# The first batch of a polysketch attention kernel: k turned without stride, v loaded by token group on two queues, remainders on 128 rows

## The chip, the core and the metric

The kernel runs on one core of a Trainium2 chip. The metric is device time in microseconds for one execution; the time given is the median of several runs. The engines are named as the profile names them: PE (TensorE; PEld for its weight loads), DVE (VectorE), ACT (ScalarE), POOL (GpSimd) and SP (SyncE, which here only issues DMAs). ACT can issue DMAs as well.

## What is computed

Attention with a polynomial sketch, and behind it a feed-forward layer with squared ReLU. There are 4 batches, 4 heads, 1088 tokens and head size 32, with 8 sketch rows.

```
def phi(x):
    a = np.einsum('rd,bhsd->bhsr', S1, x)
    b = np.einsum('rd,bhsd->bhsr', S2, x)
    return np.einsum('bhsi,bhsj->bhsij', a, b).reshape(*x.shape[:-1], r * r)
q_p, k_p = (phi(q), phi(k))
kv = np.einsum('bhsf,bhsd->bhfd', k_p, v)
z = np.sum(k_p, axis=2)
num = np.einsum('bhsf,bhfd->bhsd', q_p, kv)
den = np.einsum('bhsf,bhf->bhs', q_p, z)[..., None] + 1e-06
x = (num / den)            # to (4352, 128): a token's four heads side by side
h = np.maximum(x @ w_in, 0.0)        # 128 -> 2048
out = h * h @ w_out                  # 2048 -> 128
```

## The kernel before, in words

**The feed-forward part** sets most of the time. The 4352 tokens are cut into nine chunks: two of 512 tokens for each batch (32 rows of tokens times 16), and one of 256 for the remainders (2 tokens of each row of 34). For each chunk there are 16 steps. A step is a first product, `pg` (L938: 128 columns of w_in with xT, the normalized attention turned so that features lie on partitions), a squared ReLU shared among DVE, ACT and POOL, and a second product, `po` (L1026), summed over the 16 steps. The call `block()` (L1005) emits one first product, four steps ahead, and one second product; a block is the unit in which the code counts time, in `now`.

**The attention part** gives xT. For a batch, k and q are turned 32 by 32 on DVE (`turned`, L237), projected on the sketches (`proj` for the first batch, `proj4` for the others), and spread to 64 features by an outer product of the two factors (`outer`, on DVE or POOL). `KvRows` (L423) sums k's features with v on PE, and the sums z of the features from the factors alone (`factor_sums`). `keep_rows` (L455) copies the first from PSUM by ACT, `turn`, `place`, `pick_sums` and `own_sums` set both into the operand `kvbd` of `numerators` (L499). `normalize_first` or `normalize` divides and scales on DVE, and the result is turned on PE (x_ps) or through DRAM into xT.

**The first batch's first group** is written out by hand (L1035 to L1130), because the feed-forward part can't begin without it. Its order on each engine is the order of the code. `idle_products` are products of zeros with no use but to keep PE at work. `first_two` (L963) emits the first two first products of chunk 0.

**The loads** stand in SP's queue in the order of the code (L164 to L183). For batch 0: k in two halves (each of four groups of 128 columns), k's remainder, q's first half, v by heads (four loads to 128 partitions), q's second half, v's remainder in two loads, then w_in, w_out and batch 1. The sketches go out on ACT's queue. Each element of xt, and each partition of v_sb, stands for a set of tokens; the transposition of k writes with a stride, so that its columns agree with v's partitions. v's remainder and k's are kept for two batches in one tile, each on 64 partitions.

**Everything later** is emitted by generators, called lanes. After each block `pump` lets each lane that is due make one step. A lane holds itself back by conditions on `now`, on an estimate of when DVE and POOL are free (`dve_free`, `pool_free`), and on a flag that one buffer of PSUM is taken (`take_nd`). `second_group` makes chunk 1 (batch 0, second group); `batch_gen` makes batches 1 to 3, each with two chunks. A batch's factors of q go out to DRAM and come back as f (`factors_gen`, SP's queue). A chunk that is made more than 12 blocks ahead of its use goes through DRAM: `x<-xsT` (L643), and three blocks later four loads `xT<-x` (L649), also on SP's queue. `first_product` asks for a chunk when its first step is due: chunk c in block 16c - 2.

Of the kernel before, what the change touches and what calls it, by code (L numbers as in the profile page):

```python
# [21 lines left out]
def kernel(  # L22
# [24 lines left out]
    VONE = H * 8 * D  # L47
# [33 lines left out]
    for b in range(B):  # L81
        for x, tag in ((k_sb, "k_sb"), (q_sb, "q_sb")):
            x[b] = cpool.tile([128, NM * D], F32, name=f"{tag}{b}")
        v_sb[b] = cpool.tile([128, VONE + D], F32, name=f"v_sb{b}")
    for r in range(2):
        v_rm[r] = cpool.tile([128, H * D + D], F32, name=f"v_rm{r}")
# [33 lines left out]
    def load_v(b, h):  # L120
        sp.dma_start(  # L121
            v_sb[b][:, 256 * h : 256 * h + 256],
            bass.AP(
                v.tensor,
                v.offset + (b * H + h) * S * D,
                [[NM * D, 32], [8 * D, 4], [1, 8 * D]],
            ),
        )

    def load_v_rest(b, i):  # L130
        sp.dma_start(
            _v(v_rm[b // 2], 0, [[D, H], [1, D]], 64 * (b % 2) + 32 * i, 32),
            bass.AP(
                v.tensor,
                v.offset + (b * H * S + 32 + i) * D,
                [[NM * D, 32], [S * D, H], [1, D]],
            ),
        )
# [26 lines left out]
    load_k(0, 1)  # L165
    load_rest(k_sb[0], k, 0)
    load_q(0, 0)
    for h in range(H):
        load_v(0, h)
    load_q(0, 1)  # L170
    for i in range(2):
        load_v_rest(0, i)
# [7 lines left out]
    for i in range(2):  # L180
        load_v_rest(1, i)
# [9 lines left out]
    warm = cpool.tile([1, 2], F32)  # L191
    dve.memset(warm[:], 0.0)
    act.activation(warm[:, 1:2], warm[:, 0:1], Square)
# [9 lines left out]
    for i in range(B):  # L203
        (dve if i == 0 else pool).memset(kvbd[i][:], 0.0)
    for b in range(B):
        pool.memset(v_sb[b][:, VONE : VONE + D], 1.0)
    for r in range(2):
        pool.memset(v_rm[r][:, H * D : H * D + D], 1.0)
# [19 lines left out]
    def idle_products(n, w=512):  # L228
        idle_ps = pspool.tile([128, 512], F32, name="idle_ps", tag="po", bufs=2)
        for i in range(n):  # L230
            nc.tensor.matmul(idle_ps[:, 0:w], zero[:, 0:128], zero[:, 0:w])  # L231
# [5 lines left out]
    def turned(x, g, of_q=False):  # L237

        if g < 2:
            xt = apool.tile([128, 512], F32, tag="xt", bufs=6)  # L240
            c0, w = (512 * g, 128) if of_q else (128 * g, 256)
            dve.transpose(  # L242
                xt[:, :] if of_q else _v(xt, 0, [[128, 4], [1, 4], [4, 32]]),
                _v(x, c0, [[32, 4], [w, 4], [1, 32]]),
            )
# [108 lines left out]
    rest_ab = {}  # L354
    for r in range(2):
        rest_ab[r] = (
            cpool.tile([128, 64], F32, name=f"abr{r}"),
            cpool.tile([128, 256], F32, name=f"phr_k{r}"),
        )

    def proj_rests(xk, b, xqs, qf=None, ps_tag="ms"):
# [5 lines left out]
        for g, xt in xqs:  # L367
            nc.tensor.matmul(ab_ps[64 * g : 64 * g + 64, 64:128], w_bt[:, :], xt[:, 0:64])
        act.copy(
            _v(rest_ab[b // 2][0], 0, [[32, 2], [8, 4], [1, 8]], p0, 64),  # L370
# [6 lines left out]
    def outer_rest(b, eng, a=None):  # L377
        p0 = 64 * (b % 2)
        ab, ph = rest_ab[b // 2]
# [7 lines left out]
    def factor_sums(ps, c0, ab, a0, a1, w, p0, n, first, last):  # L387

        nc.tensor.matmul(
            ps[32 * w : 32 * w + 32, c0 : c0 + 32],  # L390
            ab[p0 : p0 + n, a0 : a0 + 32],
            ab[p0 : p0 + n, a0 + a1 : a0 + a1 + 32],
            start=first,
            stop=last,
        )
# [27 lines left out]
    class KvRows:  # L423
# [3 lines left out]
        def __init__(self, b, abs_=None):  # L427
            self.b, self.abs = b, abs_
            self.ps = pspool.tile([128, 1024], F32, name="kvr_ps", tag="nd", bufs=1)

        def values(self, ph, c0, vt, v0, v1, p0, n, first, last):
            for h in range(H):
                nc.tensor.matmul(  # L433
                    self.ps[32 * h : 32 * h + 32, 0:64],
                    vt[p0 : p0 + n, v0 + v1 * h : v0 + v1 * h + 32],
                    ph[p0 : p0 + n, c0 + 64 * h : c0 + 64 * h + 64],
# [4 lines left out]
        def tile(self, ph, g, t, last=False):  # L441
            self.values(
                ph, 256 * t, v_sb[self.b], D * (4 * g + t), 256, 0, 128, g + t == 0, last
            )

        def rest(self, last=False):
            r, p0 = self.b // 2, 64 * (self.b % 2)
            self.values(rest_ab[r][1], 0, v_rm[r], 0, D, p0, 64, False, last)

        def rest_sums(self):  # L450
            factor_sums(
                self.ps, 512, rest_ab[self.b // 2][0], 0, 32, 0, 64 * (self.b % 2), 64, False, True
            )
# [5 lines left out]
        def keep_sums(self):  # L459
            self.sums = apool.tile([128, 32], F32, name="kvz", tag="kvz")  # L460
            act.copy(self.sums[:, :], self.ps[:, 512:544])

        def products(self, phs):
            for g in range(2):
                for t in range(4):
                    self.tile(phs[g], g, t)
                for t in range(4):
                    factor_sums(
                        self.ps, 512, self.abs, 128 * g + 32 * t, 256, t, 0, 128,
                        g == 0, g == 1 and t > 0,  # L470
                    )
            self.rest(True)
# [19 lines left out]
        def spread(self):  # L492
# [4 lines left out]
            own_sums(self.b, t_ps, 64)  # L497
# [34 lines left out]
    def normalize_first(nds, xT):  # L532


        (den, rden, top, rtop, rs), (_, mp, _, beta) = norm_tiles()
        xs = apool.tile([128, 512], F16, tag="xs")
        for i, nd in enumerate(nds):
# [10 lines left out]
        dve.tensor_tensor(out=rtop[:, :], in0=top[:, :], in1=rden[:, :], op=mult)  # L548

        mm, rm = (_v(nds[1], 144 + 8 * x, [[1, 4]]) for x in range(2))  # L550
        dve.tensor_reduce(
            out=mm, in_=_v(rtop, 0, [[4, 4], [1, 4]]),
            axis=AX, op=amax, apply_absolute_value=True,
        )
        dve.tensor_scalar(
            out=mp[:, :], in0=mm, scalar1=1.0, scalar2=1.0 / 1024.0, op0=add, op1=mult,
        )
        dve.reciprocal(rm, mp[:, :])
        dve.tensor_tensor(
            out=_v(rs, 0, [[4, 4], [1, 4]]),  # L560
            in0=_v(rden, 0, [[4, 4], [1, 4]]),
            in1=_v(nds[1], 152, [[1, 4], [0, 4]]),
            op=mult,
# [8 lines left out]
        yield  # L572
        pool.tensor_tensor(out=beta[:, :], in0=mp[:, :], in1=mp[:, :], op=mult)
# [181 lines left out]
    def batch_gen(b):  # L755
# [55 lines left out]
        kv.spread()  # L811
# [223 lines left out]
    idle_products(7)  # L1035
    s_ps = pspool.tile([128, 16], F32, name="s_ps", tag="nd", bufs=1)
    nc.tensor.transpose(s_ps[:, :], s_nat[:, :], iden[0:16, 0:16])
    idle_products(4, 128)
    xk = [turned(k_sb[0], 0)]
# [5 lines left out]
    )  # L1045
    for x in range(2):
# [7 lines left out]
    phq = ph_tile("ph_q", 2)  # L1054
    xkr = turned(k_sb[0], 2)
    xq = turned(q_sb[0], 0, True)
# [5 lines left out]
    kv0 = KvRows(0)  # L1062
    for g in range(2):
        for t in range(4):
            factor_sums(kv0.ps, 512, pk[g][1], 32 * t, 128, t, 0, 128, g == 0, g == 1 and t > 0)
# [9 lines left out]
    pick_sums(zt_ps, 0, kv0.sums)  # L1075
    for t in range(4):
        kv0.tile(phk[1], 1, t)
    own_sums(0, zt_ps, 0)
    xq1 = turned(q_sb[0], 1, True)
# [17 lines left out]
    kv0.rest(True)  # L1097
    kv0.keep_rows()
    pqT = [turned_half(phq, 0, (act, act))]
# [3 lines left out]
    pqT.append(turned_half(phq, 2, (act, dve)))  # L1103
# [5 lines left out]
    pq1 = proj(xq1, "pg")  # L1109
    phq1 = ph_tile("ph_q", 2)  # L1110
    xT0 = apool.tile([128, 512], F16, name="xT", tag="xT", bufs=3)
    norm = normalize_first(nd0, xT0)
    next(norm)
    for t0 in (0, 2):
        outer(phq1, pq1[1], t0, 2, pool)
# [4 lines left out]
    idle_products(4)  # L1120
    chunk_of(0, 0, xT0, next(norm))
    first_two()
    pqT = [turned_half(phq1, 0, (act, dve))]
# [10 lines left out]
    def second_group():  # L1134
        pqT.append(turned_half(phq1, 2, (act, dve)))
        yield 1, 0
# [6 lines left out]
    lanes.append([second_group(), 1, 1])  # L1143
    add_work(*(batch_gen(b) for b in range(1, B)))
    later = []
    for b in range(2, B):
# [4 lines left out]
        later += [(n + 6 + i, load_v_rest, (b, i)) for i in range(2)]  # L1151
# [40 lines left out]
```

## Time and profile before

| | |
|---|---|
| median of 3 runs | 195.96 us (195.68 to 195.97) |
| the profiled execution | 196.73 us, its span 194.8 us |
| PE busy | 185.4 us (95%), 1380 products |
| DVE, ACT, POOL busy | 119.6, 108.2, 71.1 us |
| chain that ended last | PE 89%, SP's queue 3%, DMA 2%, ACT 2% |
| DMA in the first 20 us | share 0.85 of 16 engines, 264 GB/s |
| first second product (po, L1026) | 19.92 us |
| last one's end, PE (po_r, L985) | near 191 us |

Times inside a profile count from the first instruction of the span. A row of the timeline merges instructions of one line; its bracket gives the idle time before it and who ended it. A wait for several semaphores is put down to the one that came last by the profile. "issue" in the chain is time in which an engine waited for nothing that the profile shows.

### The profile page before, as it was taken

To read this page: it belongs to the slowest core of one execution; us is meant where nothing else is said; L and a number is where in the kernel's file an instruction comes from. 1 tells how busy PE (TensorE), PEld (TensorE's weight loads), DVE (VectorE), ACT (ScalarE), POOL (GpSimd) and SP (SyncE) were. 2 spreads that over 40 slices of the span, in tenths; PEclk is the share of its full clock that TensorE was granted. 3 is DMA by queue.
4 is the path that set the end of the run, shared out by engine and by line. 5 is a ranking of instruction groups with operands and counts; after the bars stand their busy time and mean duration, and the time that the engine had idled before them with its cause. 6 is when DMAs were issued, how large, how long until landed. Compare 5 with 4: busy or idle time off the path is not lost.

```text
span 194.8 us, 3746 instructions
## 1 busy us (share of the span) xinstructions
PE 185.4 (95%) x1380; PEld 97.2 (50%) x1380; DVE 119.6 (61%) x272; ACT 108.2 (56%) x212; POOL 71.1 (36%) x91
## 2 busy tenths in 40 slices
PE   7985999999999999999999999999999999999992
PEld 2763445454545454545454455554454444444791
DVE  4956495556487848455877545567558664644671
ACT  3235659655466755544766655457646565456570
POOL 3604122645236229242370654542524222522200
PEclk9999999999999999999999999999999999999999
DMA  6799380298913837649130349199100411300021
GB/s 170 212 347 313 107 298 25 59 242 279 228 16 108 253 69 177 192 94 280 27 54 1 52 96 263 42 227 231 29 3 0 84 30 13 54 0 2 5 52 27
DMA packets 37826, 23.17 MB, mean 119 GB/s; under 512 B 27888, under 2 KB 33264, under 8 KB 37808
## 3 DMA queue, kind: packets, MB, share of 16 engines
q1 hardware_dynamic: 37568, 22.86, 45.2%
q8 instruction: 11, 0.18, 0.4%
q14 instruction: 7, 0.06, 0.2%
q10 hardware_dynamic: 240, 0.07, 0.2%
HBM read 16.26 MB, written 6.67 MB: 118 GB/s over the span
## 4 chain that ended last, share of the span: by engine, by line
PE 89%; SPq 3%; DMA 2%; issue 2%; ACT 2%; DVE 1%; DVEq 0%
PE po L1026 56%; PE pg L938 16%; PE nd L257 4%; PE kvr_ps L433 2%; DMA v_rm<-in_v_dram 2%; PE po L985 2%; PE po_r L985 2%; PE ab_ps L257 2%; PE ab_ps L276 1%; SPq L121 1%; PE t_ps L1085 1%; PE idle_ps L231 1%; SPq L105 1%; SPq L95 0%; ACT phTh L74 0%
## 5 line engine op out<-in xcount | busy, mean ns | idle before, releaser
L1026 PE MATMUL po<-g,w_o 128*128 128x512 f32 x256 | 130.7, 592 | 0.1
L955 DVE TENSOR_SCALAR gt<-pg 128x512 f32<-128x512 f32 (+1 forms) x105 | 67.5, 647 | 50.8 <-PE pg L938 42.9
L958 ACT ACTIVATE g<-gt 128x512 f32<-128x512 f32 (+1 forms) x105 | 62.5, 597 | 60.8 <-DVE gt L955 58.8
L1026 PEld LDWEIGHTS po<-g,w_o 128*128 128x128 f32 x256 | 48.5, 191 | 39.7 <-issue 19.7
L938 PE MATMUL pg<-xT,w_in 128*128 128x512 f16 x126 | 47.7, 380 | 1.0 <-DVE own_z L409 0.8
L946 POOL TENSOR_TENSOR g<-gt 128x512 f32<-128x512 f32 x22 | 22.9, 1039 | 70.1 <-ACT gt L945 70.1
L938 PEld LDWEIGHTS <-w_in 128*128 128x128 f16 x142 | 13.9, 98 | 28.1 <-issue 27.1
L326 POOL TENSOR_TENSOR phF<-f,f 128x576 f32<-128x576 f32 (+1 forms) x12 | 16.1, 1364 | 10.7 <-DMA f<-q_two 10.7
L344 POOL TENSOR_TENSOR ph_k<-ab 128x512 f32<-128x512 f32 x14 | 14.5, 1068 | 8.9 <-ACT ab L282 7.7
L945 ACT ACTIVATE gt<-pg 128x512 f32<-128x512 f32 x22 | 12.8, 581 | 0.1
L911 POOL TENSOR_TENSOR o_sb<-oT,beta_t 128x512 f32<-128x512 f32 x8 | 8.4, 1048 | 9.7 <-DVE oT L906 4.0
L952 ACT ACTIVATE g<-gt 128x512 f32<-128x512 f32 x15 | 9.4, 630 | 0.5
L242 DVE STREAM_TRANSPOSE xt<-k_sb 128x512 f32<-128x512 f32 x8 | 8.3, 1106 | 1.4 <-DMA k_sb<-in_k_dram 1.4
L257 PEld LDWEIGHTS nd<-kvbd,phF 128*64 128x64 f32 x208 | 6.9, 137 | 4.5 <-issue 3.8
L951 ACT ACTIVATE gt<-pg 128x512 f32<-128x512 f32 x15 | 8.8, 586 | 0.0
L906 DVE STREAM_TRANSPOSE oT<-po 128x512 f32<-128x512 f32 x8 | 5.7, 717 | 4.8 <-PE po L1026 4.6
L257 PE MATMUL nd<-kvbd,phF 128*64 128x66 f32 x208 | 7.7, 224 | 0.0
L231 PE MATMUL idle_ps<-zero 128*128 128x512 f16 (+1 forms) x15 | 4.8, 477 | 2.8 <-issue 1.6
L257 PEld LDWEIGHTS ab_ps<-w_bd,xt 128*64 128x64 f32 x160 | 6.7, 155 | 1.5 <-issue 0.9
L257 PE MATMUL ab_ps<-w_bd,xt 128*64 128x64 f32 x160 | 6.8, 241 | 0.0
L985 PE MATMUL po<-w_o,g 128*128 128x128 f32 x32 | 6.2, 278 | 0.0
L985 PE MATMUL po_r<-w_o,g 128*128 128x128 f32 x32 | 6.0, 275 | 0.0
(120 smaller groups left out, 132.8 us busy)
## 6 DMA issues: line engine op xcount, KB each, us to landing
q_two<-qf SPq DMA_DIRECT2D x8, 288.0 KB
f<-q_one SPq DMA_DIRECT2D x4, 576.0 KB
f<-q_two SPq DMA_DIRECT2D x4, 576.0 KB
v_sb<-in_v_dram SPq DMA_DIRECT2D x16, 128.0 KB
out_dram<-o_sb SPq DMA_DIRECT2D x32, 64.0 KB
k_sb<-in_k_dram SPq DMA_DIRECT2D x3, 544.0 KB
q_sb<-in_q_dram SPq DMA_DIRECT2D x3, 544.0 KB
w_in<-in_moe_w_in_dram SPq DMA_DIRECT2D x2, 512.0 KB
```

Source lines behind the costliest of these rows:

```text
L257: nc.tensor.matmul(out_ps[p0 + c : p0 + c + z, c0 : c0 + w], lhsT[:, l0 + c : l0 + c + z], rhs)
L326: pool.tensor_tensor(out=ph[:, c], in0=fs[g][0][:, c], in1=fs[g][1][:, c], op=mult)
L344: eng.tensor_tensor(out=_v(ph, 256 * t0, [[64, 4 * m], [8, 8], [1, 8]]), in0=_v(ab if a is None else a, c0, [[n, 4 * m], [1, 8], [0, 8]]), ...
L938: nc.tensor.matmul(pg[:, 0:nt], w_in[:, 128 * c : 128 * c + 128], xT[:, 0:nt])
L945: act.activation(gt[:, 0:nt], pg[:, 0:nt], Relu)
L946: pool.tensor_tensor(out=g2[:, 0:nt], in0=gt[:, 0:nt], in1=gt[:, 0:nt], op=mult)
L951: act.activation(gt[:, 0:nt], pg[:, 0:nt], Relu)
L952: act.activation(g2[:, 0:nt], gt[:, 0:nt], Square)
L955: dve.tensor_scalar(out=gt[:, 0:nt], in0=pg[:, 0:nt], scalar1=0.0, scalar2=None, op0=amax)
L958: act.activation(g2[:, 0:nt], gt[:, 0:nt], Square)
L985: nc.tensor.matmul(po[r][:, 0:128], g2[:, 128 * r : 128 * r + 128], w_o[:, 128 * c : 128 * c + 128], start=c == 0, stop=c == NC - 1,)
L1026: nc.tensor.matmul(po[0][:, 0:nt], w_o[:, 128 * c : 128 * c + 128], g2[:, 0:nt], start=(c == 0), stop=(c == NC - 1),)
```

## The change

The change touches four places.

1. **Loads of batch 0.** v is loaded by m, a group of 32 partitions with all four heads, m = 0 and 1 on SP's queue and m = 2 and 3 on ACT's. k is turned without a stride to match. k's remainder goes out behind q's first half and v, and v's remainder ahead of q's second half. The activation that loads ACT's table is emitted earlier.
2. **Order of the first group.** The sketches' operand w_bd is made before k is turned. The first q half is turned before k's remainder. The sums z go to a PSUM buffer of their own. The evictions of phq's transposes are shared otherwise. xq1's projection, its outer products and the first half of its transposes go behind `first_two`; w_in is cast ahead; there are two slow idle products (float32) instead of four fast ones. The scale `mp` leaves DVE's chain; its 1.0 is a constant column in rtop_1.
3. **Remainders.** Each batch has its own tiles v_rm, abr and phr_k of 128 partitions, of which 64 hold data and the others are cleared by POOL. The products over them have 128 rows instead of 64. In `products` the value products of both groups come first.
4. **Lanes.** `second_group` starts one block later and has one more step; `own_sums` of batches 1 to 3 is a step of its own, a block after `spread` at the soonest.

The diff, cut to its core:

```diff
-    def load_v(b, h):
+    def load_v(b, m, eng=sp):
+        eng.dma_start(
+            v_sb[b][32 * m : 32 * m + 32, :],
...
+                v.offset + (b * H * S + 8 * m) * D,
+                [[NM * D, 32], [S * D, H], [1, 8 * D]],
...
     load_k(0, 0)
     load_k(0, 1)
+    load_q(0, 0)
+    load_v(0, 0)
+    warm = cpool.tile([1, 2], F32)
+    dve.memset(warm[:], 0.0)
+    act.activation(warm[:, 1:2], warm[:, 0:1], Square)
+    load_v(0, 2, act)
+    load_v(0, 1)
+    load_v(0, 3, act)
     load_rest(k_sb[0], k, 0)
-    load_q(0, 0)
-    for h in range(H):
-        load_v(0, h)
+    for i in range(2):
+        load_v_rest(0, i, sp)
     load_q(0, 1)
-    for i in range(2):
-        load_v_rest(0, i)
...
+    def clear_rest(b):
+        p0 = 64 - 64 * (b % 2)
+        for t in (v_rm[b], *rest_ab[b]):
+            pool.memset(t[p0 : p0 + 64, :], 0.0)
...
-            dve.transpose(
-                xt[:, :] if of_q else _v(xt, 0, [[128, 4], [1, 4], [4, 32]]),
-                _v(x, c0, [[32, 4], [w, 4], [1, 32]]),
-            )
+            dve.transpose(xt[:, :], _v(x, c0, [[32, 4], [w, 4], [1, 32]]))
...
-        kv.spread()
+        t_ps = kv.spread()
+        yield 1, 0
+        yield from dve_ready(1.0)
+        own_sums(b, t_ps, 64)
+        dve_time(0.6)
...
-    idle_products(7)
+    idle_products(5)
...
-    idle_products(4, 128)
-    xk = [turned(k_sb[0], 0)]
+    idle_products(2)
...
+    xk = [turned(k_sb[0], 0)]
...
+    xq = turned(q_sb[0], 0, True)
     xkr = turned(k_sb[0], 2)
-    xq = turned(q_sb[0], 0, True)
...
-    kv0 = KvRows(0)
+    kv0 = KvRows(0, None, pspool.tile([128, 32], F32, name="kvz_ps", tag="pg", bufs=2))
...
-    pqT = [turned_half(phq, 0, (act, act))]
+    pqT = [turned_half(phq, 0, (act, dve))]
+    xq1 = turned(q_sb[0], 1, True)
...
-    pqT.append(turned_half(phq, 2, (act, dve)))
+    pqT.append(turned_half(phq, 2, (act, act)))
...
-    pq1 = proj(xq1, "pg")
-    phq1 = ph_tile("ph_q", 2)
+    for c in range(2):
+        act.copy(
+            w_in[:, 512 * c : 512 * c + 512], w_in32[:, 512 * c : 512 * c + 512]
+        )
+    idle_products(2, True)
...
-    idle_products(4)
     chunk_of(0, 0, xT0, next(norm))
+    for b in range(1, B):
+        pool.memset(kvbd[b][:], 0.0)
+        clear_rest(b)
     first_two()
-    pqT = [turned_half(phq1, 0, (act, dve))]
+    pq1 = proj(xq1, "ms")
+    phq1 = ph_tile("ph_q", 2)
+    for t0 in (0, 2):
+        outer(phq1, pq1[1], t0, 2, pool)
...
     def second_group():
-        pqT.append(turned_half(phq1, 2, (act, dve)))
-        yield 1, 0
+        pqT = []
+        for t0 in (0, 2):
+            pqT.append(turned_half(phq1, t0, (act, dve)))
+            yield 1, 0
...
-    lanes.append([second_group(), 1, 1])
+    lanes.append([second_group(), 2, 1])
```

## The prediction, made before the changed kernel was run

> **What bounds the kernel now.** I read the profile page first, then the chain of waits for the start, then the engines' timelines, the waits of one window, and the windows' busy times. Between 20 and 191 us TensorE is the bound: 168.96 of 169 us busy but for one gap. A step off TensorE in that stretch is worth something only if it makes or removes such a gap. What can be won lies before 20 us. This is the chain that ended last, from the chain of waits (start us, us, what):
>
> ```profile
> 6.59 4.08 DMA v_rm<-in_v_dram
> ...
> 10.81 0.32 PE kvr_ps L433 x8
> ...
> 14.66 1.61 issue
> 16.27 1.02 PE idle_ps L231 x4
> 17.30 0.34 PE x_ps L577 x4
> 17.64 0.02 issue
> 17.66 0.30 DVE xT L76
> 17.97 0.14 issue
> 18.10 0.61 PE pg L968 x2
> ...
> 19.92 1.13 PE po L1026 x2
> ```
>
> The load of v's remainder, eleventh in SP's queue, ends late and holds the last product of the key/value sums. Later TensorE stands 1.61 us with nothing that it waits for ("issue"), and the idle products behind that gap end 0.4 us after their successors could have begun: DVE's second half of xs ends at 16.86. From 19.92 on, TensorE runs through.
>
> The one gap after 20 us, from TensorE's timeline and from SP's (start, us, engine, line, what):
>
> ```profile
> 82.06 0.36 PE L401 MATMUL kvt_ps<-kvz,pick 128*64 128x16 f32 x8
> 83.26 0.38 PE L938 MATMUL pg<-xT,w_in 128*128 128x512 f16 x1 [0.84 <-DVE own_z L409]
> ```
>
> ```profile
> 72.38 0.52 SPq L299 DMA_DIRECT2D q_one<-qf  x1
> 73.35 1.28 SPq L304 DMA_DIRECT2D q_two<-qf  x2
> 74.74 0.54 SPq L313 DMA_DIRECT2D f<-q_one  x1
> 77.92 0.35 SPq L316 DMA_DIRECT2D f<-q_two  x1
> 78.38 2.27 SPq L649 DMA_DIRECT2D xT<-x  x4
> ```
>
> The row names own_z, but pg reads only xT and w_in. In the trace, TensorE's sequencer waits there for the semaphores of four xT loads, the last of which lands at 83.13. This is block 46, the first product of the fourth chunk (b=1, g=1). Its loads stand in SP's queue behind batch 2's factor transfers, and those began when ACT made qf at 71.77. So the gap is: landing 83.26 less 71.77, 11.49 us that the transfers take, against 10.65 us of TensorE work between (71.77 to 82.42).
>
> The profiled execution took 196.73 us with a span of 194.8, so 1.9 lie outside. The median of the runs is 195.96. I forecast a difference and add it to the median.
>
> **Part 1, to the copy of the key/value rows** (ACT L457, 11.18 now). Sketches first: s_nat's second load lands at 3.36, the five idle products end near 3.3 (0.43 each in the row of seven, 3.17), so w_bd is ready near 3.9, when k's first half lands (3.87). The k transposes fall from 1.09 to the 0.71 of the q row, and the first does not stand ahead of w_bd any more. The first projection starts about 0.35 earlier.
>
> Loads: k, k, q, v, v go out on SP by 3.6, v, v on ACT. That makes the remainder of k sixth on SP instead of third. Before it lie 512 KB of k, 256 of q, 512 of v. The windows show 259 to 295 GB/s up to 4.5 us, where transfers lack no issue, and less later, where issue limits; 1.31 MB at 280 to 300 from 1.85 us is 6.2 to 6.5, and landing comes 0.3 to 0.8 after the last packet (k's first half: packets done near 2.8, landed 3.15 to 3.87). So it lands near 6.8, where it now lands at 4.84. DVE turns it (0.20) ahead of the first outer product, which begins at 7.05 instead of 6.67: 0.4 **lost**. Bounds: 6.6 (the first projection's copy on ACT) and 7.6.
>
> From there: outer product 0.69. The sums' new PSUM buffer has tag pg and waits for exactly that reader, so the sums come behind it, to 8.1 (0.33); the remainder's sums to 8.3. The value products no longer wait for the copy of the sums (0.27 now); they follow with 0.58, pick 0.34, products 0.47, remainder 0.12 and 0.25 to the copy: **10.1**. v's remainder, now issued by 5.1 instead of 7.0, lands 8 to 9, under that. Gain 1.1, with bounds 0.5 and 1.5 by those of the outer product.
>
> **Part 2, to the first hidden product** (18.10 now). From the copy to the reduction of the second numerators is 3.06 now (11.18 to 14.24). One eviction moves to DVE beside the copies of ACT that place kv; DVE's xq1 transpose (0.71) now lies in its wait; 2.8, a gain of 0.28. The dropped scale mp takes 0.21 off DVE's chain (15.48 to 15.68, L555); on POOL it is covered, as are the 12 memsets moved there (0.1 to 0.2 each, done by 15.7, before POOL's next product at 17.3). The stall at issue: proj of xq1 (32 weight loads and products) goes behind first_two, and the 1.61 stands after TensorE's 449th instruction. Of these 449 fall 32 of proj, 8 of four idle products and one load; 8 of the slow idle products, 8 of x_ps and 4 of first_two join: first_two ends near the 428th. x_ps then waits for xs alone: 17.66 becomes 17.25, gain 0.41. The two slow idle products take 4 x 0.43, end near 13.6 and delay nothing (xs ends at 14.9). Sum of parts 1 and 2: 1.1 + 0.28 + 0.21 + 0.41 = **2.0**; first po at 17.9. w_in's first half lands at 12.1 now and is cast by 14, ahead of pg; w_o's lands at 16.0, ahead of po.
>
> The page fetch itself: the trace's packets on queue 8, 16,384 bytes each, show the first starting at 13.55 for 1.18 us. TensorE goes on at 16.27. Later ones start about where instructions 705, 961, 1217 are reached, without a gap, thus a page ahead. By the same spacing the first was asked for at the 193rd, near 8.9, and lay behind loads. I take that: it comes by 16.3 again, and the 449th is reached near 16.9, inside proj(xq1). [...]
>
> **Part 3, behind the first product.** proj(xq1) fills the hole between pg and po (1.8 us) that the first four transposes of phq1 fill now; those move into the stream: +0.44 (their row at 21.05). The remainder at 128 rows saves at most what its eight products take over a quarter of a full tile of 32: 0.25 + 0.04 against 0.12 to 0.15, so 0.08 each for three batches, **-0.25**; lower bound 0, as many instructions remain. k's transposes (six of 0.38 less) and own_sums later on DVE lie beside a busy TensorE: nothing.
>
> Part 3's other side is the order. I followed the lanes' bookkeeping block by block; for the kernel before it gives x_ps of chunk 1 in block 9, proj4 of batch 2 behind block 37, xT loads behind 39, as the trace has them. After: second_group starts one block later and has one step more, so chunk 1's x_ps comes behind 11 (needed at 14), proj4 of batch 1 behind 11, chunk 2's x_ps behind 28 instead of 27 (needed at 30: ACT's copy ends 0.9 after it, one block is 1.08, just covered; 0 to 0.3), chunk 3's numerators behind 32 instead of 31, proj4 of batch 2 behind 38 instead of 37, its factor transfers behind 39 and chunk 3's loads behind 40. The key/value products follow behind 45, their spread behind 46 instead of 45. Block 46 still needs xT. The work ahead of it loses one block (1.08), the spread (0.53) and 0.1: 10.65 - 1.7 = 8.9 against the same 11.49. The gap grows from 0.84 to 2.6: **+1.75**. Bounds: 0 if transfers run 1.75 shorter, 2.0 with the copies late. From block 51 on the order is as before.
>
> Sum: -2.0 + 0.44 - 0.25 + 1.75 = -0.06, with chunk 2 taken as 0.1: 195.96 + 0.04, **196.0**. The winnings at the start are spent at the fourth chunk. Its own range, from 0.5 to 1.5 of part 1, is 195.6 to 196.6. About 0.2% (0.4 us) is what a measurement of this kernel can tell from no change.
>
> **Rivals.**
> - *The gap does not grow* (the four loads are less late, as SP's queue runs otherwise than I followed): for it, the row gives own_z as releaser, and own_sums does move; against it, pg does not read own_z. 196.0 - 1.75 = 194.3. Chance 0.15.
> - *k's remainder lands early*, 6.3: the outer product begins at 6.6, part 1 wins 1.5: 195.5. Chance 0.12. Against it, seven loads lie before it.
> - *Slower: k's remainder holds DVE.* DVE takes work in order, and the transposes stand ahead of all outer products. From a landing at 7.2 on the sum is 0.4 over the time before; at 7.7, with v's last half behind it, the products come 0.9 later: 196.9. For it, v's remainder now has single stragglers from 8.95 to 10.68. Chance 0.16.
> - *The page is asked for only at the 449th.* [...] Then it starts near 16.5 and, by the 2.7 from 13.55 to 16.27, TensorE resumes at 19.2, with 0.25 and two pg of 0.22 before po: 19.9, all of the start's gain lost, 197.9. Chance 0.10. Where the page comes only a little late, by 0.5 to 1, this is 196.5.
> - *The clock rises later.* Idle products are 0.43 apart in the first row and 0.21 (1.02 for four) in the second; the clock's record is full from 6.93. With fewer of them and holes, the half speed may last to 10: the 64-column passes, 0.97 for sixteen at 5.1 and 0.5 later, cost 1.7 more: 197.7. Chance 0.05. [...]
> - *It does not do what it says* (the gap at issue stays on the path): 196.4. Chance 0.04.
>
> The forecast keeps 0.38: of that 0.08 lies over 0.4 us below the time before, 0.24 within, 0.06 above. Faster: 0.15 + 0.12 + 0.08 = 0.35; slower: 0.16 + 0.10 + 0.05 + 0.04 + 0.06 = 0.41; within: 0.24. The range, 194.2 to 197.3, holds all cases but the late page and the late clock (0.15).
>
> **What would show it.** Outer product on DVE at 7.05 and the copy of the rows at 10.1; pg L968 at 16.1 and po at 17.9; no gap at issue before x_ps; a gap of 2.6 ahead of pg at the fourth chunk, near 81.0, with xT landing at its end. If that gap is 0.8, it is about 1.75 faster; if pg comes after 17, slower.

## The result, and the profile after

The changed kernel takes **200.89 us** (median of 4 runs, 200.44 to 201.92), the kernel before 195.97 beside it: a ratio of 1.0257, with a 95% interval of 1.0214 to 1.0300. It is slower by 4.9 us, outside the forecast range. The profiled execution took 200.89 us, its span is 199.1. Ratios leave out executions that are more than 1.5% above the fastest of their kernel, so they can lie under the quotient of two medians (most so below for the lane alone, with four of ten left out, and for all three undone, with six of ten).

The chain that ended last, at the start (start us, us, what):

```profile
0.75 2.99 DMA k_sb<-in_k_dram
...
3.75 4.78 DMA k_sb<-in_k_dram
...
8.56 0.24 DVE xt L266
8.80 0.59 DVE ph_k L359
...
10.14 1.03 PE kvr_ps L442 x32
11.17 0.55 PE zt_ps L409 x8
11.72 1.23 PE kvr_ps L442 x40
12.94 1.02 PE t_ps L1100 x4
...
14.22 0.59 PE t_ps L1100 x4
...
18.38 0.30 PE x_ps L587 x2
...
19.48 0.61 PE pg L982 x2
...
21.29 1.13 PE po L1040 x2
```

The load of k's remainder (4.78 us from issue to landing) now holds the start. The stall at "issue" ahead of x_ps has gone. And the rows between 9.4 and 13.8 are slow: four transposes t_ps take 1.02 at 12.94, and 0.59 at 14.22. That is the TensorE clock: its record is full from 13.80 on, where it was full from 6.93 before. A trace has no value of the clock ahead of its first record; that it was half until then is read from such rows.

DVE's timeline shows what waits for the loads (last bracket: idle time before, and who ended it):

```profile
7.22 0.71 DVE L260 STREAM_TRANSPOSE xt<-q_sb 128x512 f32<-128x512 f32 x1 [1.10 <-DMA q_sb<-in_q_dram]
8.56 0.24 DVE L266 STREAM_TRANSPOSE xt<-k_sb 128x64 f32<-128x64 f32 x1 [0.63 <-DMA k_sb<-in_k_dram]
8.73 1.25 DVE L359 TENSOR_TENSOR ph_k<-ab_ps,ab 128x512 f32<-128x512 f32 x2
```

The same rows in the kernel before:

```profile
5.86 0.20 DVE L251 STREAM_TRANSPOSE xt<-k_sb 128x64 f32<-128x64 f32 x1
6.00 0.71 DVE L242 STREAM_TRANSPOSE xt<-q_sb 128x512 f32<-128x512 f32 x1
6.67 0.69 DVE L344 TENSOR_TENSOR ph_k<-ab_ps,ab 128x512 f32<-128x512 f32 x1
```

The outer product begins at 8.73 instead of 6.67; the forecast was 7.05. The gap ahead of the fourth chunk, from TensorE's timeline, and the clock around it, from the busy times by windows (window, its length, then each engine's busy us and instructions; the last three columns are the granted clock, the DMA share and GB/s):

```profile
82.65 0.23 PE L397 MATMUL kvr_ps<-abr 128*32 128x32 f32 x2
85.63 0.59 PE L952 MATMUL pg<-xT,w_in 128*128 128x512 f16 x1 [2.75 <-DMA xT<-x]
86.01 1.91 PE L1040 MATMUL po<-g,w_o 128*128 128x512 f32 x2
```

```profile
82.06:85.48 3.42, 0.81 (x66) 0.70 (x54) 0.00 (x0) 0.41 (x3) 1.72 (x2) 1.00 0.37 106
85.48:88.89 3.41, 3.26 (x16) 1.66 (x17) 0.69 (x1) 0.79 (x2) 0.76 (x1) 0.50 0.31 66
```

The gap is 2.75 (forecast 2.6) and named by the xT load. Behind it stands what nobody forecast: for 3.41 us the granted clock is 0.50, and two products of po take 1.91. The clock's records in a trace lie whole multiples of this stretch apart (13.80 to 85.48 is 21 times 3.413); below it is called a window of the clock. In the kernel before, behind its gap of 0.84, the two products take 1.02:

```profile
83.48 1.02 PE L1026 MATMUL po<-g,w_o 128*128 128x512 f32 x2
```

The sum over the two spans, each product counted from the end of the one before it: the first po 1.37 later; the stretch from there to the gap 0.92 shorter (four more t_ps, +0.44; the spread of batch 2, -0.46, now behind the gap; the remainder's products, 0.49 to 0.22 for two batches; the rows of pg, 10.93 to 10.38; small rows, -0.08); the gap 1.91 longer; the stretch behind it 1.91 longer (0.76 for the spread, of which 0.30 is the half clock; 1.29 for po and pg, nearly all of it half clock; -0.13 for the remainder). Together 4.27, the difference of the spans. The half clock thus costs 1.5 to 1.6.

### The profile page after: what moved, and what is told of

Same layout as the page of the kernel before. It is cut to its first block, busy times and chain, and to the rows that moved or that the text cites. A ratio compares the mean times of both kernels' runs of the same rounds, so it can differ in the third digit from the quotient of the medians.

```text
span 199.1 us, 3755 instructions
## 1 busy us (share of the span) xinstructions
PE 189.2 (95%) x1376; PEld 99.3 (50%) x1376; DVE 117.3 (59%) x271; ACT 108.2 (54%) x212; POOL 73.4 (37%) x100
## 3 DMA queue, kind: packets, MB, share of 16 engines
HBM read 16.26 MB, written 6.67 MB: 115 GB/s over the span
## 4 chain that ended last, share of the span: by engine, by line
PE 89%; DMA 6%; DVE 2%; SPq 1%; ACT 1%; issue 0%; DVEq 0%
PE po L1040 55%; PE pg L952 15%; PE nd L272 5%; DMA k_sb<-in_k_dram 4%; PE kvr_ps L442 2%; PE po L999 2%; DMA xT<-x 2%; PE po_r L999 2%; PE ab_ps L272 2%; PE ab_ps L291 1%; PE t_ps L1100 1%; SPq L659 1%; PE kvt_ps L483 1%; PE kvt_ps L409 0%; PE kvz_ps L397 0%
## 5 line engine op out<-in xcount | busy, mean ns | idle before, releaser
L952 PEld LDWEIGHTS <-w_in 128*128 128x128 f16 x142 | 13.8, 98 | 29.6 <-issue 28.6
L341 POOL TENSOR_TENSOR phF<-f,f 128x576 f32<-128x576 f32 (+1 forms) x12 | 16.1, 1362 | 12.2 <-DMA f<-q_two 12.2
L272 PEld LDWEIGHTS ab_ps<-w_bd,xt 128*64 128x64 f32 x160 | 7.2, 163 | 3.8 <-issue 1.4
L272 PE MATMUL ab_ps<-w_bd,xt 128*64 128x64 f32 x160 | 7.7, 252 | 0.9 <-DVE xt L260 0.8
L260 DVE STREAM_TRANSPOSE xt<-q_sb 128x512 f32<-128x512 f32 x8 | 5.4, 695 | 1.1 <-DMA q_sb<-in_q_dram 1.1
L260 DVE STREAM_TRANSPOSE xt<-k_sb 128x512 f32<-128x512 f32 x8 | 5.4, 695 | 0.6 <-DMA k_sb<-in_k_dram 0.6
```

The costliest lines, as they stand in the source:

```text
L260: dve.transpose(xt[:, :], _v(x, c0, [[32, 4], [w, 4], [1, 32]]))
L272: nc.tensor.matmul(out_ps[p0 + c : p0 + c + z, c0 : c0 + w], lhsT[:, l0 + c : l0 + c + z], rhs)
L341: pool.tensor_tensor(out=ph[:, c], in0=fs[g][0][:, c], in1=fs[g][1][:, c], op=mult)
L952: nc.tensor.matmul(pg[:, 0:nt], w_in[:, 128 * c : 128 * c + 128], xT[:, 0:nt])
```

## The experiments

**The order and the gap.** Two runs move one number, in the changed kernel back and in the kernel before forward.

```
-    lanes.append([second_group(), 2, 1])      # changed kernel
+    lanes.append([second_group(), 1, 1])
```

> The changed kernel, with the second group's lane started one block earlier (1 instead of 2), nothing else. Theory (order): the 2.76 us gap ahead of chunk 3's first product is there because batch 2's factor transfers, and behind them the four xT loads, are issued one block later than before; the half clock from 85.5 to 88.9 follows from that gap. One block earlier brings the gap back to 0.8 to 0.9, the half clock goes, the front stays (first po at 21.3): 200.9 - 1.9 - 1.7 = 197.3. Rival 1 (own_sums, now later on DVE, makes the gap, as the releaser named in the trace of the kernel before would have it): gap and clock stay, 200.9. Rival 2 (the half clock has another cause than the gap): the gap goes, a half-clock window stays, 199.0.

Measured: 197.36 us, ratio to the kernel before 0.9984 (0.9943 to 1.0025). The gap fell from 2.75 to 1.55 and the clock stayed full behind it. It did not reach 0.84, and a gap of 0.64 came up at the sixth chunk (125.99). But the profiled start was different too, with the same code up to there: the clock was full from 7.31, and the first po came at 19.36 instead of 21.29. The total therefore mixes two effects; the other direction is cleaner:

```
-    lanes.append([second_group(), 1, 1])      # kernel before
+    lanes.append([second_group(), 3, 1])
```

> The kernel before, with the second group's lane started two blocks later (3 instead of 1), which by the block bookkeeping puts proj4 of batch 2 behind block 38 and the fourth chunk's xT loads behind 40, as the changed kernel has them; nothing else. Theory (order makes the gap, the gap halves the clock): the gap ahead of the fourth chunk's first product grows from 0.84 to 2.4 to 2.8, and where it fills over 1.8 of one clock window of 3.41 the clock is half for the next 3.41 us: 1.6 to 1.9 for the gap, 1.7 for the clock, 198.5 to 199.9 against 196 to 197 of before. Rival (the gap in the changed kernel comes from its later own_sums or from its v loads): gap stays 0.8 to 0.9, within 0.3 of before.

Measured: 198.78 us, ratio 1.0107 (1.0070 to 1.0145). TensorE's timeline at the gap, and the windows:

```profile
80.96 0.22 PE L389 MATMUL kvr_ps<-abr 64*32 64x32 f32 x2
83.41 0.38 PE L938 MATMUL pg<-xT,w_in 128*128 128x512 f16 x1 [2.23 <-DMA xT<-x]
```

```profile
80.97:84.39 3.42, 1.19 (x13) 0.51 (x7) 0.49 (x1) 0.30 (x2) 2.48 (x2) 1.00 0.21 43
84.39:87.80 3.41, 3.41 (x17) 1.75 (x17) 1.45 (x5) 1.39 (x4) 0.00 (x0) 0.50 0.56 121
```

Nothing of v, own_sums or the start was touched, and gap and half clock are there. The order makes the gap, and the gap halves the clock. The rival falls. The price of a half window shows in the kernel before without any edit: of its 91 executions beside these runs, 65 have a mean granted clock of 0.995 or more and a median of 196.31 us, 25 have 0.987 to 0.991 (one window at half speed is 0.009) and a median of 198.02. One execution does not fit: of the ten of this run, one kept 0.999 and took 198.09, hardly less than the six at 0.990 to 0.991 (198.20 to 198.85); no trace shows why.

**The loads and the clock at the start.** The first attempt put the loads back on SP, in the order of before, but left v by m:

```
+    load_rest(k_sb[0], k, 0)
     load_q(0, 0)
-    load_v(0, 0)  ...  load_v(0, 2, act)  load_v(0, 1)  load_v(0, 3, act)
+    for h in range(H):
+        load_v(0, h)
```

> The changed kernel, with batch 0's loads as the kernel before has them: all on SP, in the order k, k, k's remainder, q's first half, v, q's second half, v's remainder (v per head again, to all 128 partitions? no: by m' as in the change, only queue and place are undone). Theory (place in the queue): k's remainder lands near 4.9 instead of 8.53, q's first half near 6.0 instead of 7.2, so the first outer product begins at 6.7 to 6.9 instead of 8.73 and the first po comes at 17.9 to 18.8 instead of 21.29. Gap and half clock at chunk 3 stay. 200.9 - 2.5 to 3.4 = 197.5 to 198.4. Rival 1 (the clock, half until 13.8, holds the front whatever the loads do): first po not before 20.3, 199.9 to 200.9. Rival 2 (v's new layout, four loads to 32 partitions each, is the slow part): v's last load or its remainder holds the value products, first po 19.5 to 20.5, 199.1 to 200.1.

Measured: 201.02 us, 1.0198 (1.0120 to 1.0276). k's remainder landed at 6.03 (4.84 before) and q's first half only at 7.38 (5.97), with v's loads behind them in the same queue. The outer product began at 8.16, the first po came at 19.45, the gap was 3.11. The 1024-byte packets, all of them v's, took 73 ns (median), 65 in the changed kernel, 46 before. That speaks for the layout, as rival 2 has it, but not for its way: what waited was DVE for q's first half (1.6), not the value products for v. The time lies above all three forecasts.

```
-    idle_products(5)      # 7 of 512 columns
-    idle_products(2)      # 4 of 128 columns
```

> The changed kernel, with the idle products at the start as before: seven of 512 columns, then four of 128, in place of five and two of 512. Theory (idle products keep the clock's window busy): the granted clock is full from about 7 again instead of 13.8, the first products at half speed (9.4 to 13.8: 1.2 us of lost time) run full, some of that behind waits: first po 0.6 to 1.2 earlier, 199.7 to 200.3. Rival 1 (the hole of 0.8 at 8.1, where TensorE waits for the late loads, is what keeps the clock low): clock full from 13.8 as now, or full at 7 and half again later; 200.9. Rival 2 (the longer rows delay the sketch products): 201.2.

Measured: 202.33 us, 1.0311 (1.0206 to 1.0415). The clock rose at 13.74, po came at 21.54. The holes were at 5.54 (0.40) and 8.62 (1.10): rival 1, though the time lies above its 200.9.

> The changed kernel with all three: the lane one block earlier, the loads in the order of before on SP, the idle products of before. Theory: the causes add up, first po at 17.5 to 18.3, gap 0.8 to 0.9, no half clock behind 20 us: 194.0 to 195.2, thus faster than both kernels by 1 to 2. Rival (what holds the front is something else in the change, the new dependences of sums and evictions): first po at 19 or later, 195.8 to 197.

The three together: 199.07 us, 1.0025 (0.9962 to 1.0088); first po 19.33, gaps of 1.25 and 0.47. The rival's figure for po, though not for its reason: the outer product still began at 8.04, behind q's first half. The ten executions fall apart by their clock: four with a mean of 0.996 or more took 195.49 to 198.30, six with 0.979 to 0.983 took 198.90 to 199.85.

**Layout or place.** I tried to load each head to 128 partitions:

```
...
-                [[NM * D, 32], [S * D, H], [1, 8 * D]],
+                [[8 * D, 4], [NM * D, 32], [1, 8 * D]],
```

> The changed kernel with one thing different: each load of v takes one head to all 128 partitions (row 32m'+r as in the change) instead of one m' to 32 partitions. Queues, places and bytes stay. Theory (layout): the 1024-byte packets of the 32-partition loads took 65 ns (median) against 46 before; with 128 partitions they take about 46 again, q's first half lands near 6.3 instead of 7.20, k's remainder near 6.9 to 7.4 instead of 8.53, the first outer product begins at 7.1 to 7.6 instead of 8.73. Rival (only the place in the queues counts): remainder at 8.2 to 8.6, outer product at 8.4 or later. The time hangs on the clock too: with a rise at the first possible window (7.0 to 7.5) the first po would come at 18.3 and the time would be 197.9, with a rise two windows later 20.2 and 199.8; for the rival 199 to 200.9.

Measured: 204.52 us, 1.0380 (1.0260 to 1.0500). The packets took 46 ns, as the theory said, and yet DVE's row for k's remainder reads:

```profile
11.67 0.24 DVE L266 STREAM_TRANSPOSE xt<-k_sb 128x64 f32<-128x64 f32 x1 [4.90 <-DMA k_sb<-in_k_dram]
```

This edit has a fault of its own: its outermost count is 4, and the trace has four late completions for each such load (7.81 to 8.00 for one), where the change's loads, with 32 there, have sixteen (7.42 to 8.36 for the last one on SP). From 5.0 to 7.4 the share of the DMA engines was 0.3 to 0.5 in this trace, 1.06 in the changed kernel. That few engines worked on each load is the author's estimate from these counts. The run tells nothing on place. Two runs built on the same loads carry the fault too:

> The kernel with lane, loads on SP and idle products undone (first po 19.33, gaps of 1.25 and 0.47 at the fourth and sixth chunk), and v loaded per head to 128 partitions as well. Theory (layout): with the same loads in the same order as the kernel before, q's first half lands near 6.0 instead of 7.3 and the first outer product begins at 6.7 to 7.0 instead of 8.04; first po 17.9 to 18.3, 194.0 to 194.6 by the profile of the kernel with the three undone less 1.1 to 1.4. Rival (q is late for another reason, as in its own packets): 195.4 to 195.8 as without.

203.43 us, 1.0286 (1.0183 to 1.0389). q came early and the outer product at 7.13, but v itself held the value products (holes of 1.11 and 1.16), the clock rose at 17.14.

> As the run with v per head and the three undone, and besides the four xT loads of a chunk are issued one block behind x's write instead of three, so ahead of the next batch's factor transfers on SP. Theory (order on SP): the gaps ahead of the fourth chunk (1.25) and the sixth (0.47) go: 1.5 to 1.7 less than without, 192.4 to 193.0. Rival (the loads now hold SP while x's write lands, and the factor transfers, behind them, hold the features): a gap turns up later, before the numerators of chunks 4 and 6; 193.5 to 195.

211.49 us, 1.0734 (1.0654 to 1.0813), with a gap of 6.68 at 99.30. Mixed with slow v loads, it is taken up again below. The next run undoes the layout as the kernel before has it, and keeps places and queues:

```
-            dve.transpose(xt[:, :], ...)
+            dve.transpose(xt[:, :] if of_q else _v(xt, 0, [[128, 4], [1, 4], [4, 32]]), ...)
-            v_sb[b][32 * m : 32 * m + 32, :],
+            v_sb[b][:, 256 * h : 256 * h + 256],
-                [[NM * D, 32], [S * D, H], [1, 8 * D]],
+                [[NM * D, 32], [8 * D, 4], [1, 8 * D]],
```

> The changed kernel with k turned with stride and v loaded per head to 128 partitions (16 transfers of two rows each, as before), but with the places and the two queues of the change. Theory A (layout: 65 ns packets of 32-partition loads): k's remainder lands at 6.8 to 7.3, as I had forecast for the change itself, outer product at 7.1 to 7.6. Theory B (place in the queue): remainder at 8.2 to 8.6, outer product at 8.4 or later. Time by A 198.3 to 199.5, by B 200 to 201.

Measured: 198.51 us, 1.0077 (1.0038 to 1.0116). Packets 46 ns again; k's remainder landed at 7.98, the outer product began at 8.17, and with the clock full from 10.14 po came at 19.40. Between the two theories: in this pair of traces the layout is worth 0.56 at the outer product. The five traces with the change's loads and DVE's order begin it at 8.63 to 9.65, so the direction holds and the size is loose. With the order of before on SP as well, and the idle row of before:

> The changed kernel with its first part undone: k turned with stride, v loaded per head in the order of before, all of batch 0's loads on SP in the order of before, idle products of before; sketches still ahead of the first transpose, and all the rest of the change (order, remainder at 128 rows, page cover). Theory: k's remainder lands near 4.9 and q's first half near 6.0, the outer product begins at 6.7 to 7.0 instead of 8.73, and the rest of the front is as forecast: first po 17.9 to 18.6, so 2.7 to 3.4 earlier than in the changed kernel. Gap and half clock at the fourth chunk stay. 197.3 to 198.2. Rival (the sums' and evictions' new order is what costs at the front): po at 19.3 or later, 198.9 or more.

Measured: 198.56 us, 1.0077 (1.0031 to 1.0123). k's remainder landed at 4.85, q's first half at 5.70, the outer product began at 7.36, the rows' copy at 10.63, pg at 16.67, po at 18.49: inside the forecast 17.9 to 18.6; the outer product came later than forecast, and the time lies 0.4 above its forecast. Place and queue are worth 0.81 at the outer product (8.17 to 7.36). The layout shows again: in the two traces with this order of loads but v to 32 partitions it began at 8.04 and 8.16. The gap at the fourth chunk was 3.19, with the half clock. The rival (sums and evictions) falls.

**Does DVE's order hold the start?**

```
+    for g in range(2): outer(phk[g], ...)      # ahead of both
     xq = turned(q_sb[0], 0, True)
     xkr = turned(k_sb[0], 2)
```

> The changed kernel with the first outer products issued on DVE (and POOL) ahead of the transposes of q's first half and of k's remainder, nothing else. Theory (the two transposes, waiting for late loads, hold DVE): the first outer product begins at 7.0 to 7.3 instead of 8.73, as soon as its operands are copied; the value products follow 0.8 to 1.4 earlier, first po 20.0 to 20.5 if the clock rises at 13.8 as before, 18.3 if at 7.3. Time 199.7 to 200.2, or 198. Rival (the remainder's own chain, its projection and sums, ends as late and holds the copies): first po unchanged, 200.9.

```profile
6.47 0.69 DVE L359 TENSOR_TENSOR ph_k<-ab_ps,ab 128x512 f32<-128x512 f32 x1 [0.26 <-ACT ab L282]
...
8.00 0.70 DVE L260 STREAM_TRANSPOSE xt<-q_sb 128x512 f32<-128x512 f32 x1
```

The outer product does begin at 6.47, 2.3 earlier, and the first po comes at 22.27, later than in the changed kernel: 201.71 us, 1.0238 (1.0164 to 1.0313). q is turned later, TensorE stands still for 1.91 at 8.85, and the clock, full from 5.99, falls to half from 9.40 to 16.23. Both are wrong here: the theory let the clock rise once and stay, and the rival left it out.

**The clock by itself.** The changed kernel again, with nothing different:

> The changed kernel again, nothing different. Theory (the rise of the clock hangs on where the 3.41 us windows lie against the start, and that differs from run to run): the second trace has another phase; if a window that closes by 10 holds less than 0.3 of idle time the first po comes at 19.3 to 19.8, otherwise near 21.3 again; median 199 to 201. Rival (the late clock belongs to the code): full from 13.4 to 14.2, po at 21.0 to 21.6.

201.38 us, 1.0238 (1.0155 to 1.0321). In its trace q's first half landed at 8.14, TensorE stood still for 2.46, and the windows read:

```profile
5.93:9.35 3.42, 0.96 (x31) 0.85 (x30) 0.71 (x1) 0.74 (x2) 2.09 (x2) 1.00 0.66 106
9.35:12.76 3.41, 3.31 (x85) 2.79 (x84) 2.86 (x7) 0.75 (x3) 0.63 (x1) 0.50 0.89 255
```

The clock rose at 5.93, fell at 9.35 and was full from 16.18; po came at 22.73. So neither side is right as written: the moment differs from run to run, and in both traces of this code holes behind the late loads cost the clock, at another moment in each. Filling the holes:

```
-    idle_products(5)  ...  idle_products(2)
+    idle_products(6)  ...  idle_products(3)
+    idle_products(3)
     pq = proj(xq, "po")
```

> The changed kernel with more idle products where TensorE stood still at the start: 6 and 3 instead of 5 and 2, and 3 ahead of the projection of q's first half. Theory (at half speed a window of 3.41 us must hold less than some 0.3 us of idle time for the clock to rise, and the holes at 3.7, 6.2 and 8.1 break two windows): the clock is full from 7 to 10.4 at the latest whatever the window's phase, first po at 19.3 to 20.0 instead of 21.29; gap and half clock at the fourth chunk stay: 199.0 to 199.8. Rival (the late loads alone make the front): po within 0.3 of 21.3, 200.9 or more, since the added products only take time.

200.10 us, 1.0159 (1.0096 to 1.0221). The outer product began at 8.94, later than in the changed kernel, and yet po came at 19.66, 1.63 earlier, with the clock full from 5.96. Gap (2.46) and half clock at the fourth chunk as in the changed kernel. This is one trace: the other three executions have a mean clock of 0.983 where the profiled one has 0.991, so one more window at half speed, and the time lies above the forecast. "Whatever the window's phase" is not shown.

**Together, and a faster version.** Layout, loads, idle row and lane undone:

> As the run with the first part undone, and the lane one block earlier as well. Theory (causes add up): gap at the fourth chunk 0.8 to 1.5, no half clock behind 20 us, first po 17.9 to 18.6: 194.0 to 195.2, under both kernels. Rival (the earlier stream meets the transfers earlier and the gaps eat the gain): gaps over 2 in all, 196 and more.

196.46 us, 0.9974 (0.9940 to 1.0007); gap 1.13, none later, but a hole of 0.78 at 5.93, the clock full only from 9.57, po at 19.15. With 6 and 3 idle products there:

> As the run with first part and lane undone (196.46), but with 6 and 3 idle products of 512 columns ahead of the first projection, so that no hole of 0.8 stands there. Theory: the clock is full by 7.5 at any phase, first po 17.9 to 18.6 instead of 19.15, gap at the fourth chunk 1.0 to 1.5: 195.2 to 196.0. Rival (w_bd and the transposes are what is late): po 19.0 or later, no change.

196.19 us, 0.9967 (0.9933 to 1.0001). The clock was full from 5.25, and po still at 19.11: v's remainder held the last value product (0.81 at 10.88), as in the kernel before. That is the rival's figure with another cause. So the remainder went ahead of q's second half:

```
+    for i in range(2):
+        load_v_rest(0, i, sp)
     load_q(0, 1)
```

> As the run with the holes filled (196.19), but v's remainder stands ahead of q's second half in SP's queue (issued from 5.5 instead of 6.1). Theory: it lands 0.6 to 1.2 earlier, the hole of 0.81 ahead of the last key/value product goes, first po 18.2 to 18.5 instead of 19.11: 195.2 to 195.6. Rival (q's second half, one place later, or the page of instructions holds instead): po 18.9 or later, 196.0 and more.

**195.26 us, 0.9938 (0.9912 to 0.9964): faster than both kernels, by 0.6% than the kernel before.** Its start, from TensorE's timeline:

```profile
15.10 0.61 PE L588 MATMUL x_ps<-iden,xs 128*128 128x128 f16 x4 [0.34 <-DVE xs L574]
16.19 0.59 PE L983 MATMUL pg<-xT,w_in 128*128 128x512 f16 x2 [0.47 <-DVE xT L75]
...
18.01 1.12 PE L1041 MATMUL po<-g,w_o 128*128 128x512 f32 x2
```

In this run a gap of 0.78 is left ahead of the fourth chunk. Two tries at the gap put the four xT loads ahead of the factor transfers (`yield 3, 0` to `yield 1, 0` behind x's write); the first is built on the run of 196.19 (its gap 1.10), the second on that of 195.26.

> As the run with the holes filled, and the four xT loads issued one block behind x's write instead of three, so ahead of the next batch's factor transfers on SP. Theory: the gap at the fourth chunk goes (1.0 to 1.5 less), the features come 2 us later and are needed only blocks later: 194.0 to 194.9, under both kernels. Rival (SP stands waiting for x's write, and the factor transfers behind it hold POOL's features): a gap of 1 or more later, 196 or more.

205.37 us, 1.0425 (1.0321 to 1.0529): the rival. The gap went, but the beta transfers had moved ahead of the factors as well, and POOL stood on its features; from the waits, 74 to 92:

```profile
POOL phF L342 <- DMA f<-q_two: 9.8, 1, 9.8
...
PE po L1041 <- POOL g L961: 3.1, 1, 3.1
```

With beta left behind (`yield 2, 0` ahead of the return):

> As the run with v's remainder early, and the four xT loads one block behind x's write, ahead of the factor transfers, but with the two beta transfers left two blocks later, behind them. Theory: the gap at the fourth chunk (1.1) goes, the factors come 2 to 4 us later and POOL's features, due from block 45, wait up to 2.5 without holding TensorE: 194.1 to 194.5, under both kernels. Rival (POOL takes work in order, and the evictions behind the waiting feature product hold TensorE as they did with the beta transfers ahead, 3.15 at 90.9): a gap of 1 to 2 near 86 to 91, 195.5 to 198.

195.08 us, 0.9913 (0.9878 to 0.9948). POOL still waits 7.2 for f, TensorE has 0.62 of gap at 87.39 in place of 0.78 at 81.88. It cannot be told from the run before it; the queue only passes the wait on.

## Why the prediction was wrong, point by point

**Part 1 failed at its landing of k's remainder:** 6.8 forecast, 8.53 measured, and with it the outer product (7.05, 8.73). The step that failed is the bytes over a rate: 1.31 MB at 280 to 300 GB/s put the last packet at 6.2 to 6.5. In the trace the remainder's 128 packets (of 256 bytes) run from 6.50 to 7.81, and 1.44 MB had moved by then, 242 GB/s from 1.86 on. The landing came 0.72 behind the last packet, inside the 0.3 to 0.8 of the forecast. The layout is one part of it: the packets of loads to 32 partitions took 65 ns instead of 46 (0.56 at the outer product, by the run with the layout undone). The working had also let SP issue freely, which it did not; from SP's waits, 0 to 12:

```profile
SPq L103 <- DMA q_sb<-in_q_dram: 1.5, 1, 1.5
SPq L129 <- DMA k_sb<-in_k_dram: 0.8, 1, 0.8
...
SPq L111 <- DMA k_sb<-in_k_dram: 0.5, 1, 0.5
```

k's remainder was issued at 3.75, 0.01 after k's first half landed; v's second remainder at 5.40 (k's second half landed at 5.38), q's second half at 7.21 (q's first, 7.20). The landings in each case are counted by the same semaphore (102, 105 and 107 in the trace). Eight (100, 102, 103, 105 and 107 to 110) serve the loads of both queues, those of the sketches among them; k's remainder is the tenth load, and with two of v's loads on ACT's queue SP came to it before k's first half had landed. No run shows that these waits cost time: the remainder's first packet went 2.75 after its issue, and q's second half is turned only at 14.86. The rival "k's remainder holds DVE" (from a landing at 7.2) named the right place, and 196.9 was too little for it, because it went to a landing of 7.7 and left out the clock. That k's transposes fall to 0.71 and the first projection begins earlier held (sixteen products from about 4.9).

**The clock at the start** was a rival at 0.05 and 197.7; the sum put it at nothing. It is about half of the loss there: from the outer product to the copy of the rows the changed kernel takes 4.28, and from the copy to po 8.29. The same start with a rise at 7.31 (the run that moves the lane) takes 2.87 and 7.86, which is 1.84 less. The other 1.68 is the late outer product.

**Part 2 held**, once the clock was full: from the copy to po 7.85 or 7.86 in every trace whose clock is full by the copy (7.8 forecast, 8.74 in the kernel before), the change's own start among them. In the run of 195.26 the copy comes at 10.16 (10.1 forecast), pg at 16.19 (16.1), po at 18.01 (17.9); that these times agree as well is in part luck, since its loads are not those of the forecast. The gain itself is loose: in the second trace of the kernel before (the run with its lane moved) the stall at "issue" is 0.79 instead of 1.61, and the stretch takes 8.32. After the change there is no stall at "issue", the page is in time (its packet on queue 8 runs from 14.17 to 15.33, TensorE's 449th instruction starts at 20.23), mp and memsets are covered. No run shows the start near 16.5 that the rival of the late page counts with. In the changed kernel itself x_ps waits for xs alone.

**Part 3:** t_ps +0.44 (0.88 against 0.44) as forecast. The remainder's padding is worth 0.40 (0.49 to 0.22, and 0.25 to 0.11), not 0.25. The gap of 2.6 came as 2.75, by the mechanism forecast: 11.64 from qf (73.99) to pg (11.49 forecast), against 8.89 of work (8.9). The bookkeeping by blocks that gave it was borne out in the kernel before as well (2.23), and the nine traces of the changed lane have 2.41 to 3.19. What was missing is its consequence: 1.5 to 1.6 for 3.41 us at half clock. No term and no rival had it.

Sum of the misses, trace against trace: 3.4 at the start (1.68 the outer product, 1.84 the clock, -0.1 the rest), 1.5 to 1.6 for the half clock, 0.16 for the gap, -0.15 for the padding, -0.1 for chunk 2, which lost nothing, and -0.55 in the rows of pg, which nobody forecast and no run explains: 4.2 to 4.3. The spans differ by 4.27, and 0.04 was forecast. The medians differ by 4.9, because the profiled execution of the kernel before, at 196.73, lay 0.77 over its median and that of the changed kernel did not.

## What to carry to other kernels

When a load is moved, bytes over a bandwidth are not its landing: here the last packet of the load counted, at 7.81 where the sum had 6.2 to 6.5. A gap on TensorE cost twice here where it was long: behind 2.75 the half clock took another 1.5 to 1.6, behind 1.55 the clock stayed full. So a forecast of a gap has to ask how long it is, not only that it is there. A kernel that changes four things can hold a good one: here the new order of the first group gives the 7.85 from the copy to po, and the time shows it only where the loads, the layout and the lane are undone and the holes at the start are filled. No run takes the parts of that order from each other.

## What the runs showed of the hardware

**The clock's window.** Between the records of one trace lie whole multiples of 3.413 us (13.80 to 85.48 is 21 of them, the half clock lasts one). At full speed the clock fell at the end of windows with (among others) 1.76, 1.81, 2.15 (the run with DVE's order moved, from 5.99), 2.23 (the kernel before with its lane moved, from 80.97), 2.46 (the rerun, from 5.93) and 2.61 us (the changed kernel, from 82.06) of idle time, and stayed after 1.62 (the kernel before, 13.76 to 17.17) and 1.37, but also after 1.97 in one window (from 91.17 in the run of 211.49): no sharp limit shows in these readings. At half speed it rose after windows with at most 0.27 idle (the rerun, from 2.52), and not after 0.30 (the changed kernel, from 3.56), 0.39 and 0.77. Four windows do not fit, and stay open. One rise, at 3.98 in the run with all three undone, came after 0.66 of idle time. And three windows right behind a fall at the start had next to no idle time (0.10 from 9.35 in the rerun shown above, 0.13 from 9.40 in the run with DVE's order moved, 0.00 from 12.67 in the run of 211.49), and the clock stayed at half for another window. The phase of the windows against the start differs from trace to trace: counted back from the records, one begins at 0.15 in the changed kernel and at 2.52 in its rerun.

**Thirty-two partitions.** The 512 packets of 1024 bytes took 55 to 73 ns (median) in the eight traces where v went to 32 partitions a load (65 in the changed kernel), 46 in all others (the kernel before among them): 1.2 to 1.6 times as long. No run shows why.

**Eight semaphores for the loads** made SP wait 0.5, 0.8 and 1.5 us in the changed kernel, each time for an earlier load to land before it issued the next. In the kernel before, with batch 0's loads all on SP, it waited for none.
